# Deriving the sine matrices from the cosine ones, re-laying two seams, and moving an output bias to VectorE, in a fused forward and backward kernel

## The chip, the cores and the metric

The kernel runs on one core of one Trainium2 chip. The metric is the device time of one execution in microseconds (us). Each experiment was timed in alternation with the kernel before, in five rounds on one chip. The five jobs of the experiments fell on four chips (two of them on the same one), so a kernel is compared with the kernel before of its own job only. The first measurement of the change, four runs each, came before them.

## The reference

One block of a network with its gradients: a modulation vector from `c`, a spectral mixer (two-dimensional real FFT, product with weights, inverse FFT) and an MLP with GELU. Inputs and outputs are bfloat16: 2048 tokens, width 1024, hidden width 3584.

```python
mod = (silu(c) @ w_mod).reshape(c.shape[0], 6, 1, -1)      # sa, ca, ga, sb, cb, gb
h = layernorm(x) * (1 + ca) + sa
x = x + ga * irfft2(rfft2(h) * (w_r + 1j * w_i))
h = layernorm(x) * (1 + cb) + sb
x = x + gb * (gelu(h @ w1 + b1) @ w2 + b2)
# outputs: x, and its vector-Jacobian product with grad_out for nine inputs
```

The FFTs are done as matmuls with cosine and sine matrices, which the kernel makes at its start.

## The kernel before

Seven stages follow one another on TensorE: gradient transposes and modulation (`pt`, `pm`), forward spectral mixer (`pu`, `pcs`, `pv`, `po`) with `pp` matmuls as filler, MLP forward (`pz` and `pbo`), MLP backward through w1 (`pg`), the gradient of w2 (`gw2acc`), the backward spectral mixer with `gw2acc` as filler, and the gradient of w1 (`gw1acc`). Buffers with the same `tag` share memory. A builder fixes the order of every engine's instructions when the kernel is built. In the traces an instruction that waits holds up those behind it on its engine (VectorE in the changed kernel: an addition whose inputs were ready at 834.60 us started at 841.24, shown below).

Making the matrices, eight of them by the same recipe:

```python
def trig(dst, colv, rowv, nrow, width, modn, cosine):
    sh = float(3 * modn // 4 if cosine else modn // 2)
    for r in range(nrow):                                   # GpSimd: index = column * row + shift
        pts(idx[:, r * width:(r + 1) * width], colv, rowv[:, r:r + 1], sh, ALU.mult, ALU.add)
    nc.vector.tensor_scalar(out=idx[:, 0:n], in0=idx[:, 0:n], scalar1=modn - 1, op0=ALU.bitwise_and, ...)
    nc.scalar.activation(out=dst, in_=idx[:, 0:n]..., func=ACT.Sin, ...)

for cl, colv, modn in ((CE, kevc, 2048), (SE, kev, 2048), (CO, kod, 4096), (SO, kod, 4096)):
    # ... two trig calls each, then a store
```

The MLP's output pass for token block b and half h, and the end of the forward part (the first seam):

```python
for i in range(4):                                          # the bias, as one-row matmuls
    last_pe[0] = nc.tensor.matmul(pbs[i][:], lhsT=ones_bf[0:1, :], rhs=b2_row[0:1, cs_], start=True, stop=False)
# ... 7 x 16 matmuls pbo; ScalarE copies pbs into bo
tt(go, go, bo, ALU.mult)                                    # VectorE
tt(bo, bo, bcn(gb_row[:, cs_], 4), ALU.mult)
# ...
yield
# pa: column sum of go, by four matmuls with ones; added to gacc
# ...
for late in bo_late:
    next(late, None)                                        # the last column sum
store_gmod([gacc[:, 0:KH], gacc[:, KH:D]], 5)               # row 5 of the modulation gradient, to DRAM
```

The backward pass and, inside it, the "ring". The ring needs row 5 of the modulation gradient from DRAM. In eight steps it loads a block of `w_mod`, multiplies it by that row and reduces (VectorE), makes another product (VectorE) and stores it. It has three buffers, `gmw[0]`, `gmw[1]` and `gmg[0]`; the buffer of `gmw` is later that of `gwo`.

```python
early = gmod_ring((5,), [gmw[:, 0], gmw[:, 1], gmg[:, 0]], gmg[:, 1, :])
next(early)                                                 # the row and the first two blocks are loaded
for b in range(NB):                                         # 4 token blocks
    for h in range(2):
        # 112 matmuls pg; ScalarE evicts into gn3
    # ln_bwd(gn3 ...)                                       # VectorE and ScalarE, 4 times
    next(early, None)                                       # a ring step
    # sums3: column sums acc3a, acc3b of gn3 on TensorE; second ln_bwd
    next(early, None)                                       # a ring step
    # ...
    fold2_in[b] = fold_d(fbuf2[:, b], n3u[:], ftmp)
    if b < NB - 1:
        sums3_ga(b, au)
        next(early, None)                                   # a ring step
```

The gradient of w2 (the second seam):

```python
hh_load(0)
yield
hh_load(1)                                                  # transposing load
for fc in range(NFC):
    # hh_load(fc + 2)
    for h in range(2 if fc < NFC - 2 else 0):
        acc = ps_f("gw2acc")
        for t in range(NT):                                 # 16 token tiles, gB[t // 4]
            gw2_mm(acc, fc, h, t)
        gw2_out(acc, fc, h)                                 # eviction to gwo, store in GpSimd's queue
        yield
```

## Time and profile before

| | us |
|---|---|
| median of 4 runs | 1522.65 |
| lowest to highest | 1520.95 to 1526.85 |

### The profile page before, as it was taken

What the parts mean: (1) busy time and instruction counts of PE and PEld (TensorE: products, weight loads), DVE (VectorE), ACT (ScalarE), POOL (GpSimd) and SP (SyncE); (2) the same over time, 40 slices, a digit from 0 to 9 for tenths busy, and PEclk for the clock granted to TensorE, in tenths of its full rate; (3) what the DMA queues carried; (4) which work ended last, traced back from release to release, by engine and by line L of the source; (5) the groups of instructions that cost most, each with busy time, mean ns of one, the idle gap of its engine ahead of it and who ended that gap; (6) DMA issues with size and microseconds to landing.
All of it is one profiled execution on the core that took longest, in us unless ns stands there. A gap on an engine that the chain in (4) does not pass through costs nothing.

```text
span 1521.4 us, 18355 instructions
## 1 busy us (share of the span) xinstructions
PE 1437.8 (95%) x6831; PEld 667.6 (44%) x6831; DVE 1072.0 (70%) x1577; ACT 722.1 (47%) x956; POOL 363.5 (24%) x428
## 2 busy tenths in 40 slices
PE   5889899999999999999989999979998899999998
PEld 2434445444444444444334444434444444444443
DVE  5992868897799887877224977967066666898633
ACT  4765556668876666655012333322522344443211
POOL 5720621111112122220210101311033421322423
PEclk8999999999999999999999999989999999999999
DMA  9972745989587876999956336496288986766996
GB/s 327 282 207 66 198 150 176 280 258 339 193 265 238 211 254 216 257 282 271 322 170 205 135 101 221 109 275 176 63 201 225 235 242 183 197 174 163 257 206 195
DMA packets 358160, 324.27 MB, mean 213 GB/s; under 512 B 209187, under 2 KB 300849, under 8 KB 357816
## 3 DMA queue, kind: packets, MB, share of 16 engines
q1 hardware_dynamic: 324184, 207.71, 52.4%
q0 software_dynamic: 33888, 115.41, 22.5%
q8 instruction: 53, 0.87, 0.2%
q14 instruction: 35, 0.29, 0.1%
HBM read 164.15 MB, written 109.10 MB: 180 GB/s over the span
## 4 chain that ended last, share of the span: by engine, by line
PE 47%; DVE 22%; DMA 10%; issue 10%; ACT 6%; POOL 3%; SPq 1%; POOLq 0%; ACTq 0%; DVEq 0%
PE pbo L817 11%; PE pz L776 9%; PE gw2acc L1090 8%; PE pg L996 5%; DVE ct L173 4%; PE pv L544 3%; PE pu L451 3%; PE gw1acc L1157 2%; PE pp L659 2%; DVE got L895 2%; DVE fbuf L173 1%; DMA gB<-in_grad_out_dram 1%; DVE gn3a L900 1%; DMA out_dram<-otl 1%; DVE gt L173 1%
## 5 line engine op out<-in xcount | busy, mean ns | idle before, releaser
L659 PE MATMUL pp<-gBoT,wt 128*128 128x512 bf16 x896 | 200.4, 379 | 1.9 <-ACT pho L669 1.0
L1157 PE MATMUL gw1acc<-gzh,n3n 128*128 128x512 bf16 x896 | 197.0, 380 | 0.3 <-DMA gzh<-d_gz 0.3
L996 PE MATMUL pg<-w1T,gzr 128*128 128x512 bf16 x896 | 196.3, 380 | 0.4
L776 PEld LDWEIGHTS <-w 128*128 128x128 bf16 x896 | 87.7, 98 | 109.0 <-issue 3.8
L996 PEld LDWEIGHTS <-gzr 128*128 128x128 bf16 x896 | 88.0, 98 | 107.5 <-issue 2.9
L1157 PEld LDWEIGHTS <-n3n 128*128 128x128 bf16 x896 | 87.8, 98 | 104.3 <-issue 0.6
L659 PEld LDWEIGHTS <-wt 128*128 128x128 bf16 x896 | 87.4, 98 | 103.0 <-DMA wt<-in_B_w_dram 1.4
L776 PE MATMUL pz<-n3Tb,w 128*128 128x512 bf16 x448 | 99.1, 379 | 1.5 <-DVE w2sD L839 1.5
L1090 PE MATMUL gw2acc<-gB,hhsA 128*128 128x512 bf16 x448 | 100.1, 379 | 0.0
L776 PE MATMUL pz<-n3Ta,w 128*128 128x512 bf16 x448 | 98.7, 379 | 1.3 <-ACT gt L779 1.3
L817 PEld LDWEIGHTS <-hhA 128*128 128x128 bf16 x608 | 59.9, 99 | 79.0 <-issue 10.8
L1095 ACT CAST gwo<-gw2acc 128x512 bf16<-128x512 f32 x54 | 30.6, 584 | 122.4 <-PE gw2acc L1090 80.1
L779 ACT ACTIVATE gt<-pz,b_col 128x512 bf16<-128x512 f32 x112 | 72.9, 684 | 29.5 <-PE pz L776 29.0
L785 ACT ACTIVATE gt<-gt 128x2048 bf16<-128x2048 bf16 x28 | 53.4, 1910 | 64.4 <-DVE gt L173 64.4
L173 DVE TENSOR_TENSOR gt<-gt,gt 128x2048 bf16<-128x2048 bf16 x56 | 68.5, 1224 | 15.9 <-ACT gt L787 15.1
L1161 ACT CAST gwo<-gw1acc 128x512 bf16<-128x512 f32 x48 | 27.7, 584 | 109.1 <-PE gw1acc L1157 87.5
L173 DVE TENSOR_TENSOR ct<-ct 128x2048 bf16<-128x2048 bf16 x64 | 76.0, 1219 | 0.8
L1090 PE MATMUL gw2acc<-gB,hht 128*128 128x512 bf16 x256 | 58.9, 392 | 8.7 <-DVE gB L173 8.4
L1090 PEld LDWEIGHTS <-hhsA 128*128 128x128 bf16 x448 | 43.8, 98 | 50.4
L781 ACT ACTIVATE gt<-gt 128x2048 bf16<-128x2048 bf16 x28 | 53.5, 1910 | 7.6 <-DVE gb_acc L796 6.9
L787 ACT ACTIVATE gt<-gt 128x2048 bf16<-128x2048 bf16 x28 | 53.3, 1909 | 0.4
L1162 POOL DMA_DIRECT2D out_dram<-gwo x56 | 30.7, 551 | 77.9 <-ACT gwo L1161 38.3
(314 smaller groups left out, 2552.9 us busy)
## 6 DMA issues: line engine op xcount, KB each, us to landing
gzr<-d_gz SPq DMA_DIRECT2D x28, 512.0 KB, 7.7
wblk<-in_w_mod_dram SPq DMA_DIRECT2D x12, 1024.0 KB, 13.4
d_ph<-pho POOLq DMA_DIRECT2D x21, 512.0 KB, 5.2
out_dram<-otl POOLq DMA_DIRECT2D x40, 256.0 KB, 3.7
d_hh<-hhA POOLq DMA_DIRECT2D x19, 512.0 KB, 4.8
w2sD<-in_B_w_dram SPq DMA_DIRECT2D x14, 512.0 KB, 6.1
hhC<-d_ph SPq DMA_DIRECT2D x14, 512.0 KB, 5.1
w2sA<-d_ph SPq DMA_DIRECT2D x14, 512.0 KB, 4.0
```

The lines of the kernel that those rows point to most:

```text
L173: return nc.vector.tensor_tensor(out=out, in0=a, in1=b, op=op)
L451: last_pu[0] = nc.tensor.matmul(pu[:], lhsT=fb[:, i, cl, c8 * P:(c8 + 1) * P], rhs=sm[:, i, :], start=(i == 0), stop=(i == 3))
L659: last_pe[0] = nc.tensor.matmul(pp[:], lhsT=wt[:, fg % 2, cch, k * P:(k + 1) * P], rhs=gBoT[j][:, cch, :], start=(cch == 0), stop=(cch == ...
L776: last_pe[0] = nc.tensor.matmul(pz[:], lhsT=w1s[g][:, cch, k * P:(k + 1) * P], rhs=n3T[:, cch, :], start=(cch == 0), stop=(cch == NDC - 1))
L779: nc.scalar.activation(out=zb[:, k, :], in_=pz[:], func=ACT.Identity, bias=b1_col[:, fc:fc + 1], scale=1.0)
L781: nc.scalar.activation(out=av, in_=zb, func=ACT.Square)
L785: nc.scalar.activation(out=sg, in_=bv, func=ACT.Sigmoid, scale=2.0 * GK)
L787: nc.scalar.activation(out=bv, in_=bv, func=ACT.Sigmoid, scale=-2.0 * GK)
L817: last_pe[0] = nc.tensor.matmul(pbs[i][:], lhsT=hh[:, k, i * P:(i + 1) * P], rhs=wp[:, k, :], start=False, stop=(g == 6 and k == 3))
L996: nc.tensor.matmul(pgs[i][:], lhsT=gzt[g][:, k, i * P:(i + 1) * P], rhs=w1Ts[g][:, k, h * KH:(h + 1) * KH], start=(g == 0 and k == 0), sto ...
L1090: nc.tensor.matmul(acc[:], lhsT=hh_s[hh_o[fc]][:, t, :], rhs=gBs[t // 4][:, t % 4, h * KH:(h + 1) * KH], start=(t == 0), stop=(t == NT - 1))
L1157: nc.tensor.matmul(acc[:], lhsT=n3ns[t // 4][:, t % 4, cch * P:(cch + 1) * P], rhs=gz2[t // 8][:, t % 8, :], start=(t == 0), stop=(t == NT ...
```

## The change

Four parts. *Sine matrices*: row r of a sine matrix is made as row r of a cosine matrix read backwards, with alternating signs by partition, by one GpSimd multiplication ("turn") in place of index, mask and sine operations. *Output bias*: added by VectorE to the evicted output, and the column sum taken one or two groups later. *First seam*: the last column sum goes behind the first half pass of `pg`, and with it the store of row 5, the start of the ring and two buffers. *Second seam*: the first four `gw2acc` accumulators are filled chunk by chunk, with the second transposing load ahead of the `gB` loads that follow.

```diff
+    def turn(dst, mat):
+        pts(dst, mat, sgn[:], None, ALU.mult)                       # GpSimd
-        for cl, colv, modn in ((CE, kevc, 2048), (SE, kev, 2048), (CO, kod, 4096), (SO, kod, 4096)):
+        for cl, colv, modn in ((CE, kevc, 2048), (CO, kod, 4096)):
# ... trig for the cosine matrix alone
+            turn(sm[:, 1, :, c0:512], sm[:, 0, :, 511:0:-1] if c0 else sm[:, 0, :, ::-1])
# ... the output pass
-        for i in range(4):
-            with ordered():
-                last_pe[0] = nc.tensor.matmul(pbs[i][:], lhsT=ones_bf[0:1, :], rhs=b2_row[0:1, cs_], start=True, stop=False)
+        tt(bo, bo, bcn(b2_row[:, cs_], 4), ALU.add)
         tt(go, go, bo, ALU.mult)
# ...
-            if bo_late and g % 7 in (1, 2):
+            if bo_late and g % 7 == 3:
# ... the first seam
-    for late in bo_late:
-        next(late, None)
-    store_gmod([gacc[:, 0:KH], gacc[:, KH:D]], 5)
# ...
-    next(early)
# ... in the backward pass, behind the pg matmuls
+            if b == 0 and h == 0:
+                for late in bo_late:
+                    next(late, None)
+                store_gmod([gacc[:, 0:KH], gacc[:, KH:D]], 5)
+                next(early)
# ... the second seam
+        hh_load(1)
         yield
-        hh_load(1)
# ...
+            if fc == 1:
+                first = [(f_, h, (ps_s, ps_f)[f_]("gw2acc")) for f_ in range(2) for h in range(2)]
+                for b in range(NB):
+                    for f_, h, acc in first:
+                        for t in range(4 * b, 4 * b + 4):
+                            gw2_mm(acc, f_, h, t)
# ...
```

More of the change, by code (lines that the diff above doesn't have):

```diff
@@ L357 @@
     nc.gpsimd.tensor_copy(out=kevc, in_=kevi)
-    kev = gview(512, FP32)
-    nc.gpsimd.tensor_copy(out=kev, in_=kevc)
-    nc.gpsimd.memset(kev[:, 0:1], 512.0)
     kod = gview(512, FP32)
     pts(kod, kevc, 2.0, 1.0, ALU.mult, ALU.add)
+    par_i = iota([[1, 1]], 0, 1, 1)
+    nc.vector.tensor_scalar(out=par_i, in0=par_i, scalar1=1, scalar2=None, op0=ALU.bitwise_and)
+    sgn = const.tile([P, 1], FP32, name="sgn")
+    nc.vector.tensor_scalar(out=sgn[:], in0=par_i, scalar1=-2.0, scalar2=1.0, op0=ALU.mult, op1=ALU.add)
     rown = to_f(iota([[256, 4]], 1, 2, 4), 4)
@@ L367, with trig @@
     gcount = [0]
-    def trig(dst, colv, rowv, nrow, width, modn, cosine):
+    def turn(dst, mat):
+        pts(dst, mat, sgn[:], None, ALU.mult)
+    def trig(dst, colv, rowv, nrow, width, modn):
         idx = gidx[:, gcount[0] % 2, :]
         gcount[0] += 1
-        sh = float(3 * modn // 4 if cosine else modn // 2)
+        sh = float(3 * modn // 4)
         for r in range(nrow):
@@ L384, in gen_mats @@
     def gen_mats():
-        for cl, colv, modn in ((CE, kevc, 2048), (SE, kev, 2048), (CO, kod, 4096), (SO, kod, 4096)):
-            sm = (smA, smB)[cl % 2]
+        for cl, colv, modn in ((CE, kevc, 2048), (CO, kod, 4096)):
+            sm = (smA, smB)[cl]
             for i2 in range(2):
-                trig(sm[:, cl // 2, 2 * i2:2 * i2 + 2, :], colv, rown[:, 2 * i2:2 * i2 + 2], 2, 512, modn, cl < 2)
-            nc.gpsimd.dma_start(out=d_SF[:, cl], in_=sm[:, cl // 2])
-        for cl, colv, modn in ((CE, jf[:, 0:256], 1024), (SE, jf[:, 1:257], 1024), (CO, jod, 2048), (SO, jod, 2048)):
-            trig(em1[:, 0, 2 * cl:2 * cl + 2, :], colv, rowd, 2, 256, modn, cl < 2)
+                trig(sm[:, 0, 2 * i2:2 * i2 + 2, :], colv, rown[:, 2 * i2:2 * i2 + 2], 2, 512, modn)
+            c0 = 1 - cl
+            turn(sm[:, 1, :, c0:512], sm[:, 0, :, 511:0:-1] if c0 else sm[:, 0, :, ::-1])
+            if c0:
+                turn(sm[:, 1, :, 0:1], sm[:, 0, :, 0:1])
+            for k in range(2):
+                nc.gpsimd.dma_start(out=d_SF[:, cl + 2 * k], in_=sm[:, k])
+        for cl, colv, modn in ((CE, jf[:, 0:256], 1024), (CO, jod, 2048)):
+            trig(em1[:, 0, 2 * cl:2 * cl + 2, :], colv, rowd, 2, 256, modn)
+            turn(em1[:, 0, 2 * cl + 4:2 * cl + 6, :], em1[:, 0, 2 * cl:2 * cl + 2, ::-1])
         nc.gpsimd.tensor_scalar(out=em1[:, 1], in0=em1[:, 0], scalar1=2.0 / (S * D), scalar2=None, op0=ALU.mult)
@@ L745 @@
     otile = []
-    b2_row = small.tile([1, D], BF16, name="b2_row", tag="gmrow", bufs=1)
+    b2_row = small.tile([P, D], BF16, name="b2_row", tag="gmrow", bufs=1)
     def after_ph():
-        nc.sync.dma_start(out=b2_row[:], in_=B_b2.rearrange("(o n) -> o n", o=1))
+        nc.sync.dma_start(out=b2_row[:], in_=B_b2.partition_broadcast(P))
         t2, t3 = (reg.tile([P, 2, 4, BW], BF16, name=f"gt{k}", tag=f"t{k}") for k in (2, 3))
@@ L817, in bo_pass @@
                         last_pe[0] = nc.tensor.matmul(pbs[i][:], lhsT=hh[:, k, i * P:(i + 1) * P], rhs=wp[:, k, :],
-                                                      start=False, stop=(g == 6 and k == 3))
+                                                      start=(g == 0 and k == 0), stop=(g == 6 and k == 3))
             if g < 6:
@@ L832, in bo_pass @@
         yield
-        pa = (ps_d if b < NB - 1 else ps_f)("pa")
+        pa = (ps_s if b == NB - 1 and h == 1 else ps_d if b < NB - 1 else ps_f)("pa")
         for i in range(4):
@@ L955 @@
     pru = reg.tile([P, 4, D], BF16, name="pru", tag="uv3")[:]
-    got = reg.tile([P, 6, D], BF16, name="got", tag="ot")
     fbuf2 = reg.tile([P, 4, 4, D], BF16, name="fbuf2", tag="fr")
@@ L962 @@
     early = gmod_ring((5,), [gmw[:, 0], gmw[:, 1], gmg[:, 0]], gmg[:, 1, :])
-    next(early)
-    au = reg.tile([P, 4, D], BF16, name="au", tag="px1")
     fold2_in = {}
@@ L983 @@
         norm_act(n2u, n2u, 1, b)
-        go4 = got[:, 0:4, :]
-        load_tok(go4, grad_out, b)
+        if b > 0:
+            load_tok(got[:, 0:4, :], grad_out, b)
         for g in range(7):
@@ L998 @@
                                          start=(g == 0 and k == 0), stop=(g == 6 and k == 3))
+            if b == 0 and h == 0:
[3 more added lines that the diff above has]
+                next(early)
+                got = reg.tile([P, 6, D], BF16, name="got", tag="ot")
+                au = reg.tile([P, 4, D], BF16, name="au", tag="px1")
+                load_tok(got[:, 0:4, :], grad_out, b)
             for i in range(4):
@@ L1020 @@
         next(early, None)
-        tt(g2[:], g2[:], go4, ALU.add)
+        tt(g2[:], g2[:], got[:, 0:4, :], ALU.add)
         nc.gpsimd.dma_start(out=chunk_rows(d_gx1, b), in_=g2[:])
@@ L1122, in pieces @@
                 hh_load(fc + 2)
-            for h in range(2 if fc < NFC - 2 else 0):
+            if fc == 1:
[4 more added lines that the diff above has]
+                            gw2_mm(acc, f_, h, t)
+                    if b < NB - 1:
+                        yield
+                for f_, h, acc in first:
+                    gw2_out(acc, f_, h)
+                yield
+            for h in range(2 if 1 < fc < NFC - 2 else 0):
                 acc = ps_f("gw2acc")
@@ L1174 @@
     with tc.issue_after(gb_in.ins):
-        fill(6)
+        fill(8)
     for cl in (CE, SE, CO, SO):
@@ L1178 @@
     sums3(3, gn3s[1], pru)
-    fill(10)
+    fill(8)
     nc.sync.dma_start(out=em2, in_=d_E[:, 0])
```

## The prediction

> **What bounds the kernel now.** I read the page's engine totals first, then busy time by window, the matmul groups with their shapes, and last the timeline at the places where TensorE stops.
>
> The page's busy line, and three rows of the table by window (window, length, then busy time and count for each engine, then granted clock, DMA share, GB/s):
>
> ```profile
> PE 1437.8 (95%) x6831; PEld 667.6 (44%) x6831; DVE 1072.0 (70%) x1577; ACT 722.1 (47%) x956; POOL 363.5 (24%) x428
> ...
> 400.00:700.00 300.00, 297.44 (x1373) 133.33 (x1372) 255.64 (x386) 197.63 (x179) 62.64 (x68) 1.00 0.84 239
> 700.00:780.00 80.00, 71.17 (x305) 30.45 (x304) 30.13 (x43) 22.71 (x25) 11.52 (x14) 0.95 0.92 286
> ...
> 998.00:1068.00 70.00, 61.59 (x272) 26.97 (x270) 50.45 (x65) 17.67 (x23) 11.14 (x13) 0.93 0.80 201
> ```
>
> TensorE is the bound. It is 95% busy, and in the long middle stage (400 to 700 us) it lacks only 2.6 us of 300. So a change is worth the TensorE work it removes plus the TensorE idle time it closes; work moved on other engines counts only where TensorE ends up waiting for it. The window 700 to 780 and the one after 998 each lack 8 to 9 us and have a granted clock under 1: the two seams this change re-lays.
>
> A matmul of 512 columns shows 379 ns, but that is latency: the chain of waits has 32 of them in 6.91 us, so one costs 6.91/32 = 0.216 us of TensorE time. I use that figure throughout, not the 379.
>
> The first seam, in TensorE's timeline (start, length, then the idle time before and what ended it, in brackets):
>
> ```profile
> 770.46 3.62 PE L817 MATMUL pbo<-w2sB,hhA 128*128 128x512 bf16 x16
> 774.32 0.23 PE L188 MATMUL ptr<-fin,gb_bf 128*28 128x128 bf16 x1 [0.24 <-ACT otile L826]
> 778.16 1.86 PE L836 MATMUL pa<-otile,ones_bf 128*128 128x512 bf16 x4 [3.62 <-DVE otile L173]
> 779.83 35.53 PE L996 MATMUL pg<-w1T,gzr 128*128 128x512 bf16 x160
> ```
>
> The last output pass ends; its column sum (pa) must wait for the eviction and a VectorE product, 3.62 us; only then do the backward matmuls (pg) start, though their data have been there: line 996 waits for no DMA. The four pa matmuls take 1.86 us, not 1.03 as elsewhere.
>
> The second seam, where the gradient of w2 (gw2acc) begins:
>
> ```profile
> 997.21 1.02 PE L1090 MATMUL gw2acc<-gB,hht 128*128 128x512 bf16 x4 [0.25 <-issue]
> 999.38 1.02 PE L1090 MATMUL gw2acc<-gB,hht 128*128 128x512 bf16 x4 [1.16 <-DVE gB L173]
> 1005.50 1.87 PE L1090 MATMUL gw2acc<-gB,hht 128*128 128x512 bf16 x4 [5.09 <-DVE gB L173]
> 1009.52 20.29 PE L1090 MATMUL gw2acc<-gB,hht 128*128 128x512 bf16 x84 [2.15 <-DVE gB L173]
> ```
>
> Four token chunks of gB arrive one after another, and each gives only four matmuls of work, because the first accumulator needs all 16 token tiles in order.
>
> [...] after the 3.62 us gap the next eight matmuls' weight loads start about 0.42 us apart, and after the 5.09 and 2.15 us gaps ten do. [...] the existing otile products take 1.22 us. [...] a 128x2048 GpSimd scaling from 63.00 took 6.20 us, and two small VectorE operations beside it averaged 2.14 us, where the same size takes 0.42 us nearby.
>
> **The change part by part.**
>
> *Output bias.* It removes the 32 one-row matmuls of this group:
>
> ```profile
> L808 PE MATMUL pbo<-b_row,ones_bf 1*128 1x512 bf16 x32 | 8.6, 376 | 2.0 <-ACT otile L826 1.9
> ```
>
> 32 x 0.216 = 6.9 us of TensorE work. It adds 8 VectorE additions of 128x2048 bf16 at 1.22 us = 9.8 us. In 400 to 700 us VectorE is 255.6 of 300 us busy, so even with 8 to 10 us more it stays below TensorE. The column sum now comes one or two groups later, which covers the extra 1.22 us before its product. But the 8 removed matmuls of the last token block fall in 705 to 750 us, where the loads of w2 run at a DMA share near 1 and TensorE already waits for them (1.92 us for w2sC, 0.67 and 0.40 for others): the 8 x 0.216 = 1.7 us become longer waits. Net -5.2; I take -5.0.
>
> *First seam.* pg starts at once; the last pa goes behind its first half pass of 112 matmuls (24 us), when the product has long been done. Gone: 3.62 us idle, and the half clock, 8 x (0.42 - 0.216) = 1.6 us. The 0.24 us before ptr stays. PSUM allows it: the last output half uses the s and d buffers, pg the f ones. Net -5.2.
>
> *Second seam.* Two row blocks by two halves are accumulated chunk by chunk, so each chunk gives 16 matmuls, 3.46 us. Before, the first 64 matmuls end at about 1022.8 (22 are done at 1013.7 as the clock recovers, then 42 x 0.216). With the same gB times (997.1, 999.4, 1005.5, 1009.5) they would end at 1009.5 + 3.5 = 1013.0, about 1013.5 with some half clock: -9.3. But the second hidden-activation transpose now goes ahead of the fourth gB load instead of behind it. The SyncE queue issued three of these in 16.33 us, so 5.4 each, and the DMA share is 0.98 to 1.17 from 980 to 1010. If that delays the last gB by all of 5 us, 64 matmuls end at about 1019.5: -3.3. I take the middle, -6.5. The fold that feeds the next stage ended at 1055.3 on VectorE, 12.3 us before TensorE needed it at 1067.6; a gain of 9 with a delay of 5 would use that up, which is one more reason not to take -9.
>
> *Sine matrices.* 12 of 24 GpSimd index operations (median 0.69 us, about 9 to 10 us in all [...]), 6 VectorE masks (4 x 0.69 + 2 x 0.42 = 3.6 us) and 6 ScalarE sines (4 x 1.14 + 2 x 0.72 = 6.0 us) go; two GpSimd multiplications of about 2048 elements (3 to 6 us each, by the 0.73 us of a 512-element one and the 6.20 above), two of 512 and a few tiny ones come. GpSimd is even, the other two gain. All of it lies before 69 us, while the matrices are first used at 109 us and later. From 57 us on TensorE is filled with pp matmuls whenever the spectral part isn't ready, and it is 134.6 of 138 us busy in 208 to 346: an earlier fold only exchanges the order. Before 57 us its 21.6 us of idleness are mostly loads (11.5 us for w_mod). I count -1, give or take 2.
>
> Sum: -5.0 - 5.2 - 6.5 - 1.0 = -17.7; 1522.3 - 17.7 = 1504.6, stated as 1504.
>
> **The rivals.**
>
> 1. *The delayed load takes the place of the wait.* At the second seam the bound is the arrival of gB, not the order of matmuls. For it: DMA near its limit there, a 20.43 us wait on that load in the chain. Against it: the bytes are the same and the transpose is needed anyway. It would leave about 3 us of the seam: 1508, and if the fold is late too, 1510.
> 2. *VectorE becomes a bound in the middle stage.* For it: 85% busy, strictly in order, and the additions stand ahead of the GELU chain; TensorE waited 1.5 us for a VectorE eviction of pa into w2sD. Against it: less than 1.3 us at a time, twice per about 100 us. It would eat 3 to 5 us: 1508.
> 3. *GpSimd's reversed multiplications block VectorE* while the gradient transposes are evicted (29 to 45 us, TensorE waited 5.2 us there). [...] Against it: the index operations at 29.7 to 31.2 ran beside those evictions without stretching them. Worth +2 to +4.
> 4. *Everything works at its best*: 6.9 of bias and 1.5 of the ScalarE wait at 715, 5.2 and 9.3 at the seams, 3 at the start: -26, or 1496.
>
> **Range and chances.** The main rivals each cost 3 to 5 us, the best case gains 8 more; a new static order adds a few us either way. 1495 to 1513 should hold it 8 times in 10. Faster by over 2% needs under 1491.8, beyond the best case: 5%. Slower by 2% would need a wait that nothing here suggests: 1%.
>
> **What would show it.** In the changed profile: no group of one-row matmuls, and about 10 us more on VectorE in the middle stage with TensorE still 99% busy there; pg starting within 0.5 us of the last pbo at full spacing; four groups of 16 gw2acc matmuls with gaps of under 3 us, with the last gB product either at the old distance from the end of pg (12 us: the larger gain) or 5 us later (rival 1); and idle time before 57 us as before. I am wrong if the gap moves from the second seam to the first spectral matmuls after it, if new waits on VectorE appear among the pz matmuls, or if the start gains or loses more than 3 us.

## More of the kernel before

The prediction reads the page. What it does not show is how the ring ran, in VectorE's timeline of the kernel before. The columns are start, length, engine, line, operation, output from input, and in brackets the idle time before it with what ended it.

```profile
781.81 0.41 DVE L178 CAST row<-w2sD 1x512 bf16<-1x512 f32 x1
789.38 1.23 DVE L934 CUSTOM_DVE_ANT_0 gmw<-gmw,gmg 128x1024 bf16<-128x1024 bf16 x1 [7.17 <-DMA au<-d_A]
...
803.47 1.23 DVE L934 CUSTOM_DVE_ANT_0 gmw<-gmw,gmg 128x1024 bf16<-128x1024 bf16 x1 [9.26 <-DMA gmw<-in_w_mod_dram]
...
812.40 1.22 DVE L934 CUSTOM_DVE_ANT_0 gmw<-gmw,gmg 128x1024 bf16<-128x1024 bf16 x1 [4.08 <-DMA gmw<-in_w_mod_dram]
...
827.33 1.23 DVE L895 CUSTOM_DVE_ANT_0 got<-gn3a,n3u 128x1024 bf16<-128x1024 bf16 x1 [11.76 <-ACT gn3a L1001]
```

The row is finished at 782 us. Then three, three and two ring steps follow, each batch after a wait for loads of 7, 9 and 4 us. They end before 816 us. VectorE then idles 11.76 us until the first `pg` matmuls are evicted and the layer-norm chain starts at 827.33. So the ring's waits cost nothing there: VectorE had nothing else to do.

## The result, and the profile after

The changed kernel takes 1546.07 us (median of 4 runs, 1543.02 to 1546.88) against 1522.65 us. The ratio is 1.0146, 95% interval 1.0121 to 1.0171. Ratios here are the mean time of one kernel's runs over that of the other's of the same rounds, so not quite the ratio of the medians. In a later job it was 1.0069 (1.0040 to 1.0097; run e_after_again). The loss is there both times; its size, some 10 to 22 us, is not the same. The prediction said 18 us less, and it is more.

The page of the changed kernel, its line of busy times (some matmul records are missing: 6666 against 6799 weight loads), then three rows of its table by window, to be read as those in the prediction:

```profile
PE 1429.6 (93%) x6666; PEld 668.8 (43%) x6799; DVE 1083.0 (70%) x1581; ACT 717.7 (47%) x950; POOL 374.5 (24%) x420
```

```profile
400.00:700.00 300.00, 294.55 (x1337) 133.75 (x1363) 265.71 (x394) 207.52 (x187) 65.70 (x68) 0.99 0.80 238
...
780.00:998.00 218.00, 201.83 (x904) 90.57 (x922) 147.62 (x211) 67.84 (x100) 25.07 (x26) 0.98 0.45 149
998.00:1068.00 70.00, 62.79 (x278) 28.01 (x283) 50.52 (x64) 18.05 (x27) 14.01 (x14) 0.98 0.84 207
```

VectorE has 10.1 us more in the middle stage (265.71 against 255.64), as predicted, and TensorE is still busy there. The stage 780 to 998 is new among the losers. In the kernel before its row was:

```profile
780.00:998.00 218.00, 212.46 (x973) 95.07 (x971) 151.64 (x212) 64.05 (x100) 32.14 (x30) 1.00 0.51 161
```

More is seen when the span is cut at TensorE's own landmarks. I read the first and last matmul of each kind from TensorE's timeline and subtracted. Each column is the length of one stretch in us, one profiled execution per kernel:

| | to last `pp` | to last `pbo` | gap to first `pg` | to last `pg` | to first backward `pcs` | to first backward `po` | to last `gw1acc` |
|---|---|---|---|---|---|---|---|
| before | 367.1 | 407.0 | 5.8 | 217.1 | 100.0 | 168.3 | 249.8 |
| after | 378.2 | 405.4 | 0.9 | 228.1 | 103.5 | 169.2 | 249.0 |
| after, later job | 376.7 | 399.0 | 2.4 | 227.0 | 101.2 | 172.1 | 249.9 |

In the second profile the differences add up like this: start +9.6, middle with bias -8.0, first seam -3.4, `pg` stage +9.9, second seam +1.2, backward mixer +3.8, sum +13 us of a span that is 13.7 us longer. So in this profile the middle and the first seam gave about what was promised, and the start and the `pg` stage took it away. In the first profile the middle gave 1.6 us only, and this is the largest difference between the two; why is open.

The first seam, TensorE's timeline after:

```profile
784.34 0.23 PE L188 MATMUL ptr<-fin,gb_bf 128*28 128x128 bf16 x1 [0.73 <-ACT otile L833]
784.50 24.35 PE L997 MATMUL pg<-w1T,gzr 128*128 128x512 bf16 x110
808.68 1.03 PE L844 MATMUL pa<-otile,ones_bf 128*128 128x512 bf16 x4
809.55 29.95 PE L997 MATMUL pg<-w1T,gzr 128*128 128x512 bf16 x135
847.94 0.58 PE L193 MATMUL acc3a<-gn3a,sel 128*128 128x512 bf16 x1 [8.44 <-DVE gn3a L904]
848.32 0.63 PE L193 MATMUL acc3b<-gn3a,sel 128*128 128x512 bf16 x1
```

The gap before `pg` is gone. But 63 us later the first layer-norm column sum `acc3a` waits 8.44 us for VectorE. Then TensorE runs at half pace: `acc3a` to `acc3b` is 0.38 us and the matmuls after them start 0.43 us apart, where they stand 0.22 us apart in the kernel before; the granted clock was 0.50 from 842.1 to 852.3 us. Before, that wait was 0.20 us. VectorE's timeline says what it did:

```profile
820.41 1.23 DVE L938 CUSTOM_DVE_ANT_0 gmw<-gmw,gmg 128x1024 bf16<-128x1024 bf16 x1 [9.54 <-DMA gmg<-d_gmod]
...
830.03 1.23 DVE L938 CUSTOM_DVE_ANT_0 gmw<-gmw,gmg 128x1024 bf16<-128x1024 bf16 x1 [4.79 <-DMA gmw<-in_w_mod_dram]
...
836.02 1.22 DVE L899 CUSTOM_DVE_ANT_0 got<-gn3a,n3u 128x1024 bf16<-128x1024 bf16 x1
...
843.88 1.23 DVE L938 CUSTOM_DVE_ANT_0 gmw<-gmw,gmg 128x1024 bf16<-128x1024 bf16 x1 [2.48 <-DMA gmw<-in_w_mod_dram]
...
846.60 2.48 DVE L904 SCALAR_TENSOR_TENSOR gn3a<-gn3a,stats,got 128x1024 bf16<-128x1024 bf16 x2 [0.33 <-ACT got L903]
```

The ring has moved with the column sum. Its eight steps now stand ahead of and inside the layer-norm chain (lines 899 to 904), with their waits for loads, and what stands behind them on VectorE waits too: the addition that makes the chain's `sums` had its inputs from ScalarE at 834.60 us and started at 841.24, behind the ring step at 840.09 that had waited 1.45 us for its load; the operation that reads `sums` (line 901), ready at 841.40, started at 845.03, behind the ring step at 843.88 that had waited 2.48 us.

The second seam after:

```profile
1012.49 1.89 PE L1099 MATMUL gw2acc<-gB,hht 128*128 128x512 bf16 x8
1018.24 1.90 PE L1099 MATMUL gw2acc<-gB,hht 128*128 128x512 bf16 x7 [3.86 <-DMA hht<-d_hh]
...
1027.19 13.97 PE L1099 MATMUL gw2acc<-gB,hht 128*128 128x512 bf16 x63 [1.91 <-DVE gB L173]
...
1085.80 14.93 PE L461 MATMUL pu<-smA,fbuf 128*128 128x512 bf16 x55 [3.76 <-ACT U L632]
```

Less idle time while the chunks arrive, as meant: from the last `pg` to `pu` it is 67.5 us against 70.7. (The last `gB` product, though, ended 16.7 us after `pg`, against 12.5 before.) But there is a new wait at the first spectral matmuls, `pu`, for ScalarE. The waits listed for that window (engine, line, what it waited for, us in total, times, longest) show its origin:

```profile
ACT gwo L1104 <- DMA out_dram<-gwo: 15.2, 2, 10.1
POOL ws L480 <- DVE fbuf L173: 12.7, 1, 12.7
```

ScalarE's eviction into `gwo` waits for an earlier store of `gwo`. That store stands in GpSimd's queue behind gathers of `ws`, and these wait 12.7 us for VectorE. The eviction of `U`, which `pu` needs, stands behind on ScalarE.

The start after, where a turn meets VectorE:

```profile
27.48 6.17 POOL L353 TENSOR_SCALAR smA<-smA,sgn 128x2044 bf16<-128x2044 bf16 x2
...
28.66 4.81 DVE L380 TENSOR_SCALAR gidx<-gidx 128x1024 int32<-128x1024 int32 x1
...
34.39 0.34 PEld L324 LDWEIGHTS <-go 128*128 128x128 bf16 x4 [5.41 <-DVE gBoT L327]
```

The mask of the index table takes 4.81 us beside the turn instead of its usual 0.69, and TensorE's transposes wait 5.41 us behind it. (The row of GpSimd merges two multiplications: one of 5.45 us, then a small one. The mask ends 0.54 us after the long one.)

### The profile page after: what moved, and what is told of

It is laid out like the page before. It is cut to its first block, busy times and chain, and to the rows that moved or that the text cites. A ratio compares the mean times of both kernels' runs of the same rounds, so it can differ in the third digit from the quotient of the medians.

```text
span 1541.1 us, 18136 instructions
## 1 busy us (share of the span) xinstructions
PE 1429.6 (93%) x6666; PEld 668.8 (43%) x6799; DVE 1083.0 (70%) x1581; ACT 717.7 (47%) x950; POOL 374.5 (24%) x420
## 4 chain that ended last, share of the span: by engine, by line
PE 33%; DVE 26%; issue 18%; DMA 10%; ACT 6%; POOL 3%; SPq 2%; another core or an unknown queue 0%; POOLq 0%; DVEq 0%; ACTq 0%
PE pbo L824 8%; PE gw2acc L1099 6%; PE pz L786 5%; DVE gt L173 4%; DVE ct L173 3%; PE pv L554 3%; PE pu L461 3%; PE pg L997 2%; PE gw1acc L1177 2%; DVE fbuf L173 2%; ACT ct L451 2%; DVE got L899 1%; DMA xt<-d_gx 1%; DVE x L173 1%; DVE st L427 1%
## 5 line engine op out<-in xcount | busy, mean ns | idle before, releaser
L160 POOL DMA_INDIRECT out_dram<-otile,xu x16 | 21.9, 1372 | 126.0 <-DMA out_dram<-otile 25.9
```

## The experiments

Eighteen runs of changed kernels, all correct. First each part alone, then combinations, then the repair of what was found. Where a diff says "the change", the hunks are those shown above.

### Each part alone

Edits: the kernel before with one part's hunks each: the sine matrices (e_gen_only; in the profile after, the two large turns took 5.45 us each and the mask behind the first of them 4.81), the bias (e_bias_only), the first seam (e_seam1_only), the second seam (e_seam2_only). One job, one chip.

> The kernel before with the sine-matrix part alone. Theory: [...] the VectorE mask behind them takes near 5 us, the first pp matmul comes at about 49 us instead of 44.9, the store that frees the index tile comes 6 to 9 us later, and TensorE then waits some 7 us for wt: +8 to +12 us, about 1532. Rival (my prediction): the start is hidden, -1 give or take 2, about 1521.

> The kernel before with the bias on VectorE and the later column sum alone. Theory: -5 us (24 of 32 one-row matmuls at 0.216 us), about 1517. Rival: the extra VectorE work turns into waits of the pz matmuls and gives it back: 0 to +3, about 1523.

> The kernel before with the first seam alone (last column sum, row 5 store and its ring moved behind the first pg half pass). Theory: the seam itself closes (-5 us), but the ring's row arrives some 24 us later, its VectorE products stand in front of the layer-norm chain and wait for their loads, and acc3a waits 8 to 9 us for gn3a: net +3 to +7, about 1527. Rival (my prediction): -5, about 1517.

> The kernel before with the second seam alone (first two row blocks accumulated chunk by chunk). Theory: the second transpose goes ahead of the last two gB loads on the SyncE queue and delays them, so the seam gains 3 us at most, and the first pu matmuls wait 3 to 4 us for evictions behind a held GpSimd queue: -1 to +2, about 1522. Rival (my middle): -6.5, about 1516.

| | median us | ratio, 95% interval |
|---|---|---|
| e_gen_only | 1531.73 | 1.0024 (0.9999 to 1.0049) |
| e_bias_only | 1526.88 | 1.0012 (0.9994 to 1.0030) |
| e_seam1_only | 1527.10 | 1.0001 (0.9986 to 1.0016) |
| e_seam2_only | 1528.62 | 1.0011 (0.9991 to 1.0031) |

The kernel before had a median of 1526.39 in this job. No part gains anything that is clear of the noise. This already speaks against four good parts that merely disturb each other.

*First seam alone.* The gap before `pg` falls from 5.8 to 0.1 us, and the `pg` stage grows from 217.1 to 225.5 us. `acc3a` waits 6.88 us for `gn3a`. The theory for the next runs: the ring's steps, now in the chain, give back what the seam gained.

*Second seam alone.* The last `pg` to the first backward `pu` is 64.5 us instead of 70.7, and 6 us are gained. Then comes the wait for ScalarE:

```profile
1065.14 15.18 PE L451 MATMUL pu<-smA,fbuf 128*128 128x512 bf16 x56 [3.43 <-ACT U L622]
```

From there to `pcs` it takes 35.9 us instead of 29.4. Together it is 100.4 us, against 100.0 before.

*Sine part alone.* Here the same mask did not collide. This is its timeline:

```profile
27.48 0.69 DVE L380 TENSOR_SCALAR gidx<-gidx 128x1024 int32<-128x1024 int32 x1 [0.54 <-POOL gidx L353]
27.54 6.26 POOL L353 TENSOR_SCALAR smA<-smA,sgn 128x2044 bf16<-128x2044 bf16 x2
```

The instruction lists of this kernel and of the changed one agree up to here. What differs is 1.2 us in the start of the mask: at 27.48 it is 0.06 us ahead of the turn and takes 0.69 us; at 28.66 it is behind it and takes 4.81. The gradient transposes' evictions beside the same turn kept their 0.75 us. (The turn's row merges two again, 5.95 and 0.31 us.) Of the six profiles with the turn on GpSimd this is the only one without the collision; in the other five the mask took 4.32 to 4.92 us. Yet the last `pp` was late here too, at 372.4 us against 367.1.

*Bias alone.* The last `pp` to the last `pbo` falls from 407.0 to 401.1 us, so TensorE's work is really gone. But the gap to `pg` grows from 5.8 to 9.0 us. The added operation is not hidden in the last pass: `pa` waits 4.88 us instead of 3.62. The other 2 us are a wait of `ptr`, a small matmul in front of it, for ScalarE's eviction of the last pass, 0.24 us before:

```profile
770.09 0.23 PE L188 MATMUL ptr<-fin,gb_bf 128*28 128x128 bf16 x1 [2.25 <-ACT otile L823]
```

```profile
768.33 1.24 ACT L441 ACTIVATE n2u<-n2u,stats 128x1024 bf16<-128x1024 bf16 x1 [20.77 <-DMA n2u<-d_x]
```

The first eviction stands in ScalarE's list behind this layer norm, which waits for its load: a pass that ends earlier waits longer. All eight profiles with the bias part have this wait of `ptr` (0.7 to 4.3 us, in seven of them put down to ScalarE's eviction); in the twelve without it, it is at most 0.4 us. That the load is its cause is read from the traces, where it ends the norm's own wait in seven of the eight; no run moved the norm.

The backward mixer takes 174.8 us instead of 168.3; part of this is a `gw2acc` that waits for ScalarE:

```profile
1235.30 0.59 PE L1088 MATMUL gw2acc<-gB,otl 128*128 128x512 bf16 x1 [4.85 <-ACT gwo L1093]
```

ScalarE stood waiting 14.5 us for the load of `xt`, with the eviction of `gwo` behind it; in the kernel before the same wait was 8.6 us and TensorE did not feel it.

### Combinations

Edits: the change without the sine part (e_no_gen), both seams alone (e_two_seams), and the whole change with the turn on VectorE (e_turn_vec), whose diff is

```diff
     def turn(dst, mat):
-        pts(dst, mat, sgn[:], None, ALU.mult)
+        nc.vector.tensor_scalar(out=dst, in0=mat, scalar1=sgn[:], scalar2=None, op0=ALU.mult)
```

> The change without its sine part (bias, first seam and second seam kept). All four together cost 1.46% (22 us), the sine part alone 0.24%. If the parts simply added up, taking the sine part out would leave a ratio to the kernel before of 1.012. If the collision of GpSimd's sign multiplications with VectorE at the start is what costs in combination (first pp matmul 4.3 us late, first pz matmul 10.6 us late in the changed kernel), the ratio falls to 1.005 to 1.008, and the first pz matmul is back at 346 +- 1.5 us.

> Both seams re-laid, no bias part and no sine part. If the seams are independent, the ratio is that of the two alone, 1.0001 and 1.0011, so 1.001 +- 0.002. If the two seams cost something only together (they share the queue of SyncE and the buffers behind the tile of the output gradient), it is 1.005 or more, and the stretch from the last pg matmul to the first backward pu grows beyond the 70.7 us of the kernel before.

> The whole change, with the five sign multiplications on VectorE instead of GpSimd. If GpSimd's long operations holding VectorE up are the cost of the sine part (a 128x1024 int32 mask took 4.81 us instead of 0.69 beside one), the start is back to within 2 us of the kernel before (first pz at 346 to 349 us instead of 357) and the ratio falls from 1.0146 to 1.007 to 1.010. If the late release of the table that feeds the sines is the cost instead, GpSimd being out of it brings that forward too; if neither, the ratio stays at 1.0146 +- 0.002.

e_no_gen gave 1.0061 (1.0026 to 1.0096), e_two_seams 1.0010 (0.9974 to 1.0047) and e_turn_vec 1.0072 (1.0043 to 1.0101). At that time the whole change stood at 1.0146, and the drop to 1.0072 looked like the turn's doing. It was not: in the next job the unaltered change read 1.0069.

Edits of that job: none (e_after_again), and the change without the bias part (e_gen_seams).

> The changed kernel once more, unaltered, as the reference of this chip. The loss of 1.46% should come again (1.012 to 1.018). Of interest is the start of its trace: if the 10.6 us by which the first pz matmul was late is what the order of the instructions fixes, the mask of the index table again stands beside GpSimd's sign multiplication (about 4.8 us instead of 0.69) and the first pz matmul is at 354 us or later. If it was a matter of one execution, pz starts at 349 to 353 us, as in the run with the sine part alone, and the loss of time must be found elsewhere.

> Sine part and both seams, without the bias part. Known: both seams 1.001, sine part alone 1.0024, bias and both seams 1.0061, all four 1.0146. If sine part and seams only add, it is 1.003 to 1.005, and the interplay sits between the sine part and the bias part. If the sine part costs more in company of the seams, it is 1.008 or more.

e_after_again gave 1.0069 (1.0040 to 1.0097), below the range that I expected, and e_gen_seams 1.0072 (1.0045 to 1.0099). So the 15 us that the four parts seemed to cost only together were mostly a difference between two sets of runs. My theory of a strong interplay fell; what remains, 1.007 against a sum of the single parts of 1.005, is inside the intervals. In e_after_again the mask again stood behind the turn, at up to 4.85 us, and the last `pp` came at 376.7 us. With the turn on VectorE the first `pp` was back at 45.3 us (49.1 in the change, 44.9 before) and the last at 371.7, yet the end did not move. The collision is shown at the start; that it costs anything at the end is not shown. Nor is it what makes the last `pp` late: that was 371.7 us with the turn on VectorE, 372.4 us in e_gen_only without a collision, and 371.4 us in e_gen_ring332 (below) with a mask of 4.92 us.

### The ring, four placements

The rival to the ring theory: whatever moves the ring costs elsewhere what it saves, because VectorE has no free place. All on top of the first seam alone.

First attempt: no step in the first block, and the steps of block b held until the fold of block b-1.

```diff
+    def ring(b):
+        if b > 0:
+            with tc.issue_after(fold2_in[b - 1].ins):
+                next(early, None)
# ... the three next(early, None) of a block become
-        next(early, None)
+        ring(b)
```

> The first seam alone, but its eight ring steps (VectorE work that waits for weight loads) held back until the block before has been folded, so that none stands in the first block's layer-norm chain. If those steps gave the seam's gain back (acc3a waited 6.9 us for gn3a in the run with the first seam alone, pg stage 225.5 us against 217.2), the wait goes, the pg stage is 218 to 221 us and the ratio 0.995 to 0.998. If something else held gn3a up, the wait stays over 5 us and the ratio 1.000 +- 0.0015.

Ratio 1.0100 (1.0068 to 1.0132): worse. The wait of `acc3a` was gone and the `pg` stage 217.2 us, as expected. But the last ring step ran at 1027 us. It kept the buffer of `gmw`, which is that of `gwo`, and TensorE paid for it:

```profile
1034.44 43.47 PE L1096 MATMUL gw2acc<-gB,hht 128*128 128x512 bf16 x188 [14.23 <-ACT gwo L1101]
```

Second attempt: four steps in the second and four in the third block, held behind the same folds.

```diff
+    def ring(b):
+        rung[0] += 1
+        if b in (1, 2):
+            with tc.issue_after(fold2_in[b - 1].ins):
+                for _ in range(2 if rung[0] % 3 == 1 else 1):
+                    next(early, None)
```

> The first seam alone again, with the eight ring steps placed four in the second and four in the third block, so that their buffer is free before the second seam (held over to the fourth block they kept the gw2 output buffer and cost 14.2 us there). If the ring steps in the first block's chain gave the seam's gain back, the pg stage is 217 to 220 us (225.5 with the first seam alone), the second seam is back at about 100 us from last pg to first backward pcs, and the ratio is 0.994 to 0.998. If moving them always costs elsewhere what it saves, the ratio is 0.999 or more.

Ratio 1.0048 (1.0020 to 1.0076). With three buffers the fourth step has to wait for its load (two waits, 8.5 us in total), and the wait was in the chain again, now in the second block. The `pg` stage was 225.4 us:

```profile
889.30 0.59 PE L193 MATMUL acc3a<-gn3b,sel 128*128 128x512 bf16 x1 [4.74 <-DVE gn3b L896]
```

Third attempt: three, three and two steps, directly behind the folds of the first three blocks. No batch is larger than the number of buffers, and the last one stands behind the fold of the third block.

```diff
         if b < NB - 1:
             sums3_ga(b, au)
-            next(early, None)
+            with tc.high_priority():
+                with tc.issue_after(fold2_in[b].ins):
+                    for _ in range((3, 3, 2)[b]):
+                        next(early, None)
# ... the other two next(early, None) of a block go
```

It was run with the first seam alone (e_ring332), with the whole change (e_all_ring332), with the change without its sine part (e_no_gen_ring332), and with both seams and another repair (e_seams_fixed, below).

> The first seam alone, with the ring steps set right behind the fold of the first, second and third block (three, three, two, so that no step has to wait for a load: three buffers). Three placements so far: in the first block's chain (pg stage 225.5 us, seam's gain gone), three in each later block (217.2 us, but the last step at 1027 us kept the gw2 output buffer), four and four (225.4 us: the fourth waited for its load in the chain). If the ring steps in the chain are the whole of what took the first seam's gain, the pg stage is 217 to 219 us, the second seam 100 to 103 us, and the ratio 0.994 to 0.998.

> The whole change with the ring steps behind the folds as in the run before this. The whole change stands at 1.0069 [1.004, 1.0097] on the last chip. If the ring costs it 10 us in the pg stage (227 against 217), the stage is 217 to 219 us and the ratio falls by 0.004 to 0.007, to 1.000 to 1.003. If the stretch behind it gives that back, as it did in both earlier placements, the ratio stays above 1.005.

> Bias part and both seams without the sine part, with the ring steps behind the folds. Without that placement it was 1.0061 (pg stage 226.7 us, backward spectral stage 177 us against 168). If both the sine part's late start and the ring are what turned the predicted gain into a loss, this is the best of the versions that keep the bias part: 0.996 to 1.001. If the backward stage keeps its 8 us, 1.000 to 1.003.

| | with the change's ring | ring behind the folds | `pg` stage, us |
|---|---|---|---|
| first seam alone | 1.0001 (0.9986 to 1.0016) | 0.9937 (0.9910 to 0.9964) | 225.5, then 217.1 |
| bias and both seams | 1.0061 (1.0026 to 1.0096) | 0.9981 (0.9953 to 1.0009) | 226.7, then 217.2 |
| the whole change | 1.0069 (1.0040 to 1.0097) | 0.9993 (0.9963 to 1.0023) | 227.0, then 217.2 |

Three times the `pg` stage loses 8 to 10 us, and three times the ratio falls by 0.006 to 0.008, some 10 to 12 us. (The two columns are from different chips, each against the kernel before of its own job; the stage lengths come out alike on all of them.) TensorE and VectorE in e_ring332:

```profile
827.23 0.38 PE L193 MATMUL acc3a<-gn3a,sel 128*128 128x512 bf16 x1 [0.20 <-DVE gn3a L896]
```

```profile
799.94 0.41 DVE L178 CAST row<-w2sD 1x512 bf16<-1x512 f32 x1
821.54 1.22 DVE L891 CUSTOM_DVE_ANT_0 got<-gn3a,n3u 128x1024 bf16<-128x1024 bf16 x1 [21.18 <-ACT gn3a L1002]
```

Nothing stands between the row and the chain any more; the chain starts when ScalarE delivers. The last ring step ran at 1004 us, 13 us after the last `pg`, and the second seam was still 99.9 us. The rival falls with this, as far as the traces go: against e_seam1_only the `pg` stage is 8.3 us shorter, and the second seam and the backward mixer together are 0.9 us longer. By its ratio the first seam with this ring is worth some 10 us. Only the 5.6 us of the closed gap are seen in the trace; the rest is not explained. The three ratios of the right column come from one job, and the two kernels with this ring in the next job, on another chip, gained nothing (below: 1.0005 and 1.0048, with `pg` stages of 218.8 and 217.2 us). So the shorter stage is shown on two chips, the gain at the end on one.

### The second seam's new wait

Edit, on top of the second seam alone (e_seam2_store): the first four stores of `gwo` are issued by ScalarE. In e_seams_fixed the same edit, both seams, and the ring behind the folds.

```diff
         if h == 1:
-            nc.gpsimd.dma_start(out=out_6[fc * P:(fc + 1) * P, :], in_=gwo[:, fc % 2])
+            (nc.scalar if fc < 4 else nc.gpsimd).dma_start(out=out_6[fc * P:(fc + 1) * P, :], in_=gwo[:, fc % 2])
```

> The second seam alone, with the first four gw2 output stores issued by ScalarE instead of standing in GpSimd's queue behind the weight gathers. In the run with the second seam alone pu waited 3.4 us for ScalarE, whose gwo eviction waited 10 us for that store, and the stretch from the first backward pu to pcs took 35.9 us against 29.4. If this wait is what gave the seam's 6 us back, that stretch is 29.4 to 31 us and the ratio is 0.995 to 0.998. If the transposed loads are the limit, the ratio stays at 1.001 +- 0.002.

> Both seams with their repairs: ring steps behind the folds, first gw2 stores issued by ScalarE; no sine part, no bias part. The second seam with the stores alone gave 0.9985. If the two repairs add up to what the seams were meant to give (5 us and 3 to 9 us), the ratio is 0.991 to 0.996. If the idle time only moves on to the backward stage, it is 0.997 or more.

e_seam2_store gave 0.9985 (0.9955 to 1.0016). The stretch from the first backward `pu` to `pcs` is 29.4 us again, so the origin of that wait is shown. But the time went back into the chunks:

```profile
1023.30 8.57 PE L1090 MATMUL gw2acc<-gB,hht 128*128 128x512 bf16 x32 [2.67 <-ACT gwo L1095]
```

The edit itself made this new wait. ScalarE, with the four evictions of the chunks one after another and the store between them (ACTq is its issue of a transfer); below it the same four in e_seam2_only:

```profile
1018.37 1.05 ACT L1095 CAST gwo<-gw2acc 128x512 bf16<-128x512 f32 x2
1019.44 3.17 ACTq L1097 DMA_DIRECT2D out_dram<-gwo  x1
1022.66 1.07 ACT L1095 CAST gwo<-gw2acc 128x512 bf16<-128x512 f32 x2 [3.25 <-issue]
```

```profile
1019.84 2.02 ACT L1095 CAST gwo<-gw2acc 128x512 bf16<-128x512 f32 x4
```

In e_seam2_only four evictions at once took 2.02 us and no matmul waited. With the store on ScalarE its issue took 3.17 us (4.20 in e_seams_fixed) and held back the other two. Last `pg` to first backward `pcs` is 99.5 us. Over nine profiles with this seam (those with the store edit left out) that stretch averages 100.4 us, over seven without it (two failed ring placements left out) 100.2. e_seams_fixed gave 0.9942 (0.9917 to 0.9967), no different from e_ring332 of the same job. As built, the second seam is worth nothing here, with or without this edit. A store from a third queue was not tried, so what the seam would be worth with a free repair is open.

### Bias and sine part on the repaired seam

Edits: e_ring332 with the bias part, and e_ring332 with the sine part.

> The bias part on top of the first seam with the ring steps behind the folds (0.9937 without the bias part). In all profiles the stretch from the last pp to the last pbo is 402 us on average with the bias part and 405.6 without, but the bias part alone read 1.0012. If the middle stage's 3.6 us reach the end where the last pass is hidden by the first seam, the ratio is 0.990 to 0.992. If they are lost again behind it (the stretch from the first backward pcs to po was 3.4 us longer on average with the bias part), it is 0.993 to 0.997.

> The sine part on top of the first seam with the ring steps behind the folds (0.9937 without the sine part). With the sine part the last pp ended at 372 to 378 us, without it at 366 to 371. If these 4 to 7 us reach the end, the ratio is 0.996 to 0.999 and the mask beside GpSimd's sign multiplication takes about 4.8 us; if the filler matmuls take them up, it is 0.993 to 0.995.

Ratios 1.0005 (0.9976 to 1.0034) and 1.0048 (1.0017 to 1.0079), against 0.9937 of e_ring332 on another chip. Both are worse than I expected in either case. The traces explain only a part: in e_bias_ring332 the gap to `pg` is 2.5 us again instead of 0.2 and `pbo` waits 5.3 us for a load of w2. The trace of e_gen_ring332 is of its fastest execution (1523.62 us, the others 1528 to 1538), so it does not show what the longer ones lost. What these two parts cost is therefore given below as ranges. e_ring332 and e_seams_fixed are the versions that beat the kernel before, by 0.6% in the one job that they ran in.

## Why the prediction was wrong

*First seam, -5.2.* "pg starts at once" held: the gap fell from 5.8 us to 0.1 to 0.6 us in the eight profiles that have the seam without the bias part. The step that failed is the next one: "the last pa goes behind its first half pass [...], when the product has long been done". I asked what `pa` needs and not what needs `pa`. The row that it completes feeds the ring, whose loads I had never looked up in the profile. The ring lost the idle time of VectorE that it had lived in and went into the chain: 217 us became 224 to 229 us for the `pg` stage in the seven profiles with the change's ring, +9 on average, shown by taking it out again three times. In place of -5.2 this part measured about 0, and about -10 with the ring behind the folds, in one job.

*Sine matrices, -1.* The step that failed is "I count -1": it had the wrong sign. In seven profiles with the sine part the last `pp` ended at 371.4 to 378.2 us (mean 374.1), in thirteen without it at 366.3 to 370.6 (mean 368.0): +6 in place of -1. "GpSimd is even" failed too: the index operations and turns took 24.9 us there, against 18.5 us of index operations before. Rival 3 named an effect that does occur, but the wrong victim, and I dismissed it on that ground: the evictions ran beside GpSimd unharmed (0.75 us beside the turn), the mask did not (0.69 us when it started 0.06 us ahead of the turn, in e_gen_only; 4.81 when it started 1.18 us behind, in the changed kernel). The two differ in two ways. The evictions also write out a sum, the mask does not; and the evictions read PSUM, where the mask reads SBUF. No run tells whether either of them makes the difference, or why the order matters. (In the prediction's own case, "averaged 2.14 us" hid that one operation took 3.87 us and the other 0.41.) At the end of the kernel the part measured +0.24% alone and +0.12% (e_all_ring332 against e_no_gen_ring332), each on one chip, so 2 to 4 us, inside the intervals; across chips up to 17. The collision is not the cause of the late `pp`, as shown above: without it the last `pp` is just as late. So the cause of the +6, and what of it reaches the end, stays open.

*Output bias, -5.0.* The matmuls went and the middle stage became shorter: 402.2 us on average over eight profiles against 405.6 over twelve, -3.5. That VectorE would not bound the stage was right, and so was its 10 us. The step that failed is at the end of the stage: "The 0.24 us before ptr stays". It was 0.7 to 4.3 us in all eight profiles, 2.0 on average, mostly a wait for ScalarE's eviction behind a layer norm, and with it the gap to `pg` was 2 us longer (4 with the seam open). With the seam open "which covers the extra 1.22 us" is not true of the last pass either, where `pa` waited 1.3 us longer. Behind that the backward mixer was 2 us longer on average, with overlapping ranges; that is not settled. On one chip each, the part measured +0.12% alone, +0.5% added to both seams, and 0.0% added to seams and sine part: 0 to +8 us in place of -5.

*Second seam, -6.5.* The chunks behaved as worked out, somewhere between the full gain and rival 1: 6 us earlier at `pu` in e_seam2_only (last `gB` product 13.3 us after `pg`), but 3 us in the changed kernel (16.7 us, nearly rival 1). The middle of -9.3 and -3.3 is -6.3, not -6.5. Then came true what I had put down myself as a sign of error: the gap moved "from the second seam to the first spectral matmuls after it". The step that failed is the one that took the fold on VectorE as the next limit, with 12.3 us in hand; the next limit was ScalarE, through a buffer of two whose store sat in another engine's queue, and when the store was put in ScalarE's own queue, through its issue between the evictions. In place of -6.5 the part measured +0.1%, about +2.

*The chances and the range.* That the time changed by less than 2% was forecast rightly, but by luck: the sign was wrong. The range 1495 to 1513 missed because its worst case took waits of 3 to 5 us, each inside the stage that the change touches. "a new static order adds a few us either way" was the term to look at: what the ring, the layer norm on ScalarE and the store on GpSimd cost lies there.

*Half clock.* In the kernel before, the granted clock was 0.50 from 778.2 to 781.5 us, after the 3.62 us wait, and again from 1004 to 1013 us, around the waits of 5.09 and 2.15 us. In the changed kernel it was 0.50 from 842.1 to 852.3 us: after the 8.44 us wait ten matmuls in a row started about 0.43 us apart instead of 0.22, so this wait cost about 2 us more than its length (an estimate, 10 x 0.21).

## What to carry to other kernels

Before moving an operation out of a gap, follow its result forward as well as its inputs back: whatever hangs on it moves along, and the idle time it used to fill is part of its price. Work that waits for loads belongs in an engine's list only where nothing urgent stands behind it (here it cost the `pg` stage 8 to 10 us in three comparisons), and in batches no larger than its buffers (with a fourth step on three buffers `acc3a` waited 4.74 us in e_ring44). Measure each part alone and on the same chip; here the same two kernels differed by 1.5% in one set of runs and by 0.7% in another.
